# A convolution stem's forward and backward on one core: the planned order of all engines made anew, with leads by chunk

## The chip, the cores and the metric

The kernel runs on one core of a Trainium2 chip. Its time is the device time of one execution in microseconds; of several runs the median counts.

## What is computed

The reference is a strided convolution, a group norm per channel over time, a gelu, and the gradients of all four inputs:

```python
B, T, D, K = 2, 16000, 256, 31;  s = 2;  L = (T - K) // s + 1        # L = 7985
h = sum(jnp.einsum('blc,cd->bld', x[:, i:i + s * L:s, :], w[i]) for i in range(K))
mu = h.sum(1) / L;  var = ((h - mu) ** 2).sum(1) / L
out = gelu((h - mu) / sqrt(var + 1e-5) * gn_gamma + gn_beta)          # tanh form
# returned: out, and the gradients of x, w, gn_gamma, gn_beta for a given grad_out
```

x, w and all results are bfloat16; sums are kept in fp32 in PSUM.

## The kernel before

**The arithmetic.** The sums of products over 31 taps aren't done tap by tap. Taps and positions are split in halves, two and in places three times, and of each split three products are made instead of four or more: of sums or differences of the inputs ("branches" A, B_ and C_, then "leaves" A, B_ and C_). So VectorE forms sums of x, of the gradient and differences of weights, TensorE multiplies, and the shared B_ results are spread to the others in PSUM by VectorE and ScalarE.

**The stages.** F0 and F1: the forward convolution of batch 0 and 1, in four chunks of time c = 0 to 3. Per chunk there are three units (branches). A unit uses two of four PSUM tiles of two banks (`ring`), so its results must be evacuated before the unit after the next begins. `f_three_b` (L616) multiplies, ScalarE copies the product to the other halves of the tile, `f_three_ac` (L634) accumulates on it. `f_seed` (L728) is the VectorE (and for B_ ScalarE) step that adds the B_ results before the last leaves (`f_leaf`, L600) accumulate; `f_evac` (L695) is ScalarE's evacuation with sums for the norm (L711). `f_sums` (L557) holds VectorE's input sums (`tt`, L561), `w_sub` (L549) the weight differences (L551). In F1 the gelu of batch 0 runs beside (`gelu_unit`, L947 on; L956 to L980). G0 and G1: the input gradient of batch 0 and 1, again four chunks, each in two halves of three units, with `g_three_b`, `g_leaf`, `g_three_ac` (all issue from L1162), sums in `g_sums` (L1121), seeds in `g_seed` (L1211; `ve` is L676), and ScalarE's `g_evac` (through `keep`, L691). Beside it run the gelu of batch 1 (in G0), the elementwise gradient (`e_comp`, L1052 on) and differences of the gradient for the weight gradient (`d2_piece`, `sub` L1357), which go to device memory and come back. W: the weight gradient in nine combinations n = 0 to 8 (COMBOS). For each, x tiles of 1 MB are loaded (`x_raw`; two of them added to one, `x_tile`, for some n), gradient tiles come from `d2d` (`d_tile`), and VectorE sums two tiles of x (`w_add`, L1413, also used by `x_tile`), sums pairs of positions (`pair_x`, L1508), forms differences (`pair_d` L1516, `leaf_d` L1587) and spreads products (`w_both`, L1540); TensorE runs `w_pairs`, `w_single` and `w_leaf`, all through L1447. For n = 3 ScalarE's kept products are also stored to `pcd`. For n = 4 the x tiles are made by adding those of n = 2 and n = 3; for n = 5 by adding as well; for n = 6 each of four tiles is two loads and one addition.

**What sets the order.** Nothing is issued while the kernel is being described. Each call of `add` puts an operation in a list: its engine, an assumed duration, what it reads and writes, and its kind (stage, helper and caller, such as "W w_add x_tile"). `Plan.order` (L181) then gives each operation a due time: going backwards, the earliest due time of its users, or its own place on TensorE's axis, less its duration and less a lead that a table holds for its kind. A positive lead makes an operation due earlier. `Plan.listing` (L199) walks through time with a model of the engines and DMA queues and, whenever an engine is free, takes the ready operation that is due first. TensorE may look 13 operations ahead. The result is one fixed order for each engine: TensorE, VectorE (DVE), ScalarE (ACT), GpSimd (POOL) and SyncE (SP), whose order is that of almost all DMA transfers. `emit` (L323) issues all operations in that order and pins them. On the chip each engine takes its instructions in this order and waits for what each one needs.

## Time and profile before

| | |
|---|---|
| median of 3 runs | 1185.56 us (1185.14 to 1185.71) |
| profiled execution, first to last instruction | 1187.8 us |
| TensorE matmul busy | 1149.0 us |
| VectorE busy | 1047.6 us |
| ScalarE busy | 570.0 us |
| mean granted TensorE clock | 0.996 |
| moved by DMA | 255.17 MB, mean 215 GB/s |

The profile is of one execution; for it there is only the span from the first to the last instruction, which is 2.2 us longer than the median time of the unprofiled runs. PE is TensorE's matmul, PEld its weight loads (which overlap), DVE VectorE, ACT ScalarE, POOL GpSimd, SP SyncE. A row of the list of waits tells who waited, for whom, how long in total, how often, and the longest. A row of the timeline has the start, the busy time, engine, line and operation, output and input, how many, and in brackets the idle time ahead of it with what ended it. A row of a stretch has its bounds and length, the busy time and count for PE, PEld, DVE, ACT and POOL, then the granted TensorE clock, the DMA engines' mean busy share and GB/s.

### The profile page before, as it was taken

The numbers are of one execution on the slowest core, as the hardware profiler recorded it, in microseconds if no ns is written. First come the engines' busy times: TensorE is split into PE (matmuls) and PEld (weight loads), VectorE is DVE, ScalarE is ACT, GpSimd is POOL, SyncE is SP. The second block draws the span as 40 slices with busy tenths as digits, with TensorE's granted clock in tenths as the row PEclk, the third lists the DMA queues.
The fourth block names the chain that finished last, engine by engine and source line by source line (L and its number), as shares of the span: only waits on it lengthen the run. The fifth ranks groups of instructions, "written<-read, shape, count | busy, mean of one in ns | idle before, by whom it ended". The sixth has DMA issues, their size and how long they took to land.

```text
span 1187.8 us, 19338 instructions
## 1 busy us (share of the span) xinstructions
PE 1149.0 (97%) x7739; PEld 763.5 (64%) x7796; DVE 1047.6 (88%) x1358; ACT 570.0 (48%) x873; POOL 18.9 (2%) x67
## 2 busy tenths in 40 slices
PE   5999999999999999999999999999999999989998
PEld 3888889777777964444444444444488656656685
DVE  7997898799999989999879997788889898777995
ACT  1254454788885578978884476433322212111200
POOL 0000000000000000000000000000000000000000
PEclk9999999999999999999999999999999999999999
DMA  9446949968986799567639998697998824986774
GB/s 212 73 115 122 200 121 182 205 146 204 204 209 124 270 353 252 167 225 186 221 115 292 270 329 265 161 318 266 317 235 266 271 90 151 359 300 198 239 219 140
DMA packets 334100, 255.17 MB, mean 215 GB/s; under 512 B 187500, under 2 KB 312682, under 8 KB 325738
## 3 DMA queue, kind: packets, MB, share of 16 engines
q1 hardware_dynamic: 333818, 253.93, 76.6%
q8 instruction: 61, 1.00, 0.3%
q14 instruction: 29, 0.24, 0.1%
q0 software_dynamic: 192, 0.00, 0.0%
HBM read 118.95 MB, written 89.62 MB: 176 GB/s over the span
## 4 chain that ended last, share of the span: by engine, by line
PE 46%; DVE 14%; DMA 6%; issue 4%; ACT 1%; SPq 0%; DVEq 0%; ACTq 0%
PE ps L1162 27%; PE ps L1447 15%; PE ps L596 4%; DVE arena L1413 3%; DMA arena<-in_x_dram 2%; DMA arena<-dnd 2%; DVE arena L1357 2%; DVE arena L1587 2%; DVE ps L676 1%; DVE arena L676 1%; DVE arena L1516 1%; DVE arena L1508 1%; DMA dnd<-arena 1%; DVE arena L1121 1%; DVE ps L1540 1%
## 5 line engine op out<-in xcount | busy, mean ns | idle before, releaser
L1162 PE MATMUL ps<-arena 128*128 128x512 bf16 x1974 | 429.7, 376 | 6.6 <-DVE ps L676 3.6
L596 PE MATMUL ps<-arena 128*128 128x256 bf16 (+4 forms) x3460 | 408.2, 281 | 17.8 <-DVE arena L551 7.1
L596 PEld LDWEIGHTS <-arena 128*128 128x128 bf16 x3460 | 338.1, 99 | 87.7 <-DVE arena L551 7.5
L1162 PEld LDWEIGHTS <-arena 128*128 128x128 bf16 x2016 | 197.3, 98 | 237.7 <-issue 6.8
L1447 PE MATMUL ps<-arena 128*128 128x256 bf16 (+1 forms) x2305 | 312.1, 298 | 10.5 <-DVE arena L1508 7.3
L1447 PEld LDWEIGHTS <-arena 128*128 128x128 bf16 x2320 | 228.1, 98 | 94.6 <-DVE arena L1508 8.7
L691 ACT ACTIVATE arena<-ps 128x1024 f32<-128x1024 f32 (+1 forms) x143 | 145.7, 1020 | 285.3 <-PE ps L1447 98.1
L561 DVE TENSOR_TENSOR arena<-arena 128x1087 bf16<-128x1087 bf16 (+3 forms) x211 | 175.5, 866 | 13.7 <-PE ps L596 12.4
L968 DVE TENSOR_TENSOR arena<-arena 128x1024 bf16<-128x1024 bf16 x160 | 107.0, 683 | 8.5 <-ACT arena L962 3.9
L1413 DVE TENSOR_TENSOR arena<-arena 128x4096 bf16<-128x4096 bf16 x38 | 86.3, 2284 | 20.8 <-DMA arena<-in_x_dram 19.5
L1121 DVE TENSOR_TENSOR arena<-arena 128x516 bf16<-128x516 bf16 (+3 forms) x176 | 83.6, 506 | 8.6 <-PE ps L1162 8.0
L676 DVE TENSOR_TENSOR ps<-ps,arena 128x1024 f32<-128x1024 f32 x60 | 73.1, 1224 | 7.9 <-PE ps L1447 4.5
L1357 DVE TENSOR_TENSOR arena<-arena 128x768 bf16<-128x768 bf16 (+3 forms) x112 | 65.4, 636 | 9.9 <-DMA arena<-dnd 4.7
L711 ACT ACTIVATE arena<-ps 128x512 bf16<-128x512 f32 (+1 forms) x64 | 36.9, 578 | 70.4 <-PE ps L596 67.9
L676 DVE TENSOR_TENSOR ps<-arena,ps 128x1024 f32<-128x1024 f32 x44 | 53.8, 1223 | 9.3 <-PE ps L1162 5.5
L1532 ACT COPY ps<-ps 128x256 f32<-128x256 f32 x54 | 19.3, 357 | 78.7 <-PE ps L1447 77.6
L1587 DVE TENSOR_TENSOR arena<-arena 128x2304 bf16<-128x2304 bf16 x36 | 47.4, 1348 | 4.8 <-PE ps L1447 4.8
L1516 DVE TENSOR_TENSOR arena<-arena 128x1024 bf16<-128x1024 bf16 x76 | 48.7, 682 | 1.6 <-DMA arena<-d2d 1.6
L551 DVE TENSOR_TENSOR arena<-arena 128x2048 bf16<-128x2048 bf16 (+1 forms) x52 | 49.8, 989 | 0.0
L958 DVE SCALAR_TENSOR_TENSOR arena<-arena 128x1024 bf16<-128x1024 bf16 x32 | 39.0, 1219 | 11.3 <-ACT arena L956 11.1
L1189 ACT ACTIVATE ps<-ps 128x512 f32<-128x512 f32 x48 | 27.9, 582 | 41.1 <-PE ps L1162 38.0
L1508 DVE TENSOR_TENSOR arena<-arena 128x2048 bf16<-128x2048 bf16 x38 | 45.3, 1216 | 1.2 <-PE ps L1162 1.2
(79 smaller groups left out, 632.8 us busy)
## 6 DMA issues: line engine op xcount, KB each, us to landing
arena<-in_x_dram SPq DMA_DIRECT2D x40, 1024.0 KB, 9.8
arena<-d2d SPq DMA_DIRECT2D x16, 1216.0 KB, 11.5
out_dram<-arena SPq DMA_DIRECT2D x14, 1024.0 KB, 4.4
d2d<-arena SPq DMA_DIRECT2D x30, 384.0 KB, 7.1
arena<-dnd SPq DMA_DIRECT2D x10, 960.0 KB, 5.8
vl<-arena SPq DMA_DIRECT2D x36, 256.0 KB, 3.3
arena<-vl SPq DMA_DIRECT2D x9, 1024.0 KB, 6.8
hd<-arena SPq DMA_DIRECT2D x8, 1024.0 KB, 5.0
```

The source lines that it names most:

```text
L561: lambda: nc.vector.tensor_tensor(out=o, in0=a, in1=b, op=ALU.add))
L596: yield nc.tensor.matmul(ps[:, dh, cs], lhsT=wt, rhs=mv, start=s0, stop=False, skip_group_check=True)
L676: add("DVE", dve(1024, 1), [out], [a, b], lambda: nc.vector.tensor_tensor(out=out, in0=a, in1=b, op=op))
L691: lambda: nc.scalar.activation(out=out, in_=ps, func=ACT.Copy, scale=scale))
L968: add("DVE", dve(1024), [o], [a, b_], lambda: V.tensor_tensor(out=o, in0=a, in1=b_, op=op))
L1121: lambda: nc.vector.tensor_tensor(out=o, in0=a, in1=b, op=ALU.add))
L1162: yield nc.tensor.matmul(ps[:, e, 0:wide], lhsT=lt, rhs=mv, start=s0, stop=False, skip_group_check=True)
L1357: lambda: nc.vector.tensor_tensor(out=out, in0=a, in1=b_, op=ALU.subtract))
L1413: add("DVE", dve(4096), [o], [a, b], lambda: nc.vector.tensor_tensor(out=o, in0=a, in1=b, op=ALU.add))
L1447: yield nc.tensor.matmul(ps[:, s, c0:c1], lhsT=lt, rhs=mv, start=s0, stop=False, skip_group_check=True)
L1516: add("DVE", dve(1024), [d4[:, j]], [d], lambda j=j, o=o, st_=st_: nc.vector.tensor_tensor(out=d4[:, j], in0=d[:, o:o + 3 * st_ + 1:st_, : ...
L1587: add("DVE", dve(2304), [DL[i3, b]], [D2[b]], lambda b=b, i3=i3, o_=o_: nc.vector.tensor_tensor(out=DL[i3, b], in0=D2[b][:, o_:o_ + 17:2, ...
```

## The change

The table of leads is replaced, and a second one, `fine`, is added: for a kind of work it holds further leads by part. The part is the chunk c in the forward pass and the input gradient and the combination n in the weight gradient; it is set in the three loops and noted with every operation. The due time is lessened by both leads. The operations, their durations in the planner, their data and their engines are as before; only the order that `listing` makes of the due times is another.

```diff
         self.lead = {
-            "F0 f_mm f_three_ac": -2.5,
-            "F0 f_mm f_three_b": -4.0,
...
+            "F0 w_sub f_first": -3.5,
+            "F0 w_sub w2_part": -16.5,
...
+            "G1 ve g_seed": 7.0,
...
-            "W w_add x_tile": 3.0,
-            "W w_both weight_grad": 9.0,
...
+            "W load d_tile": -11.0,
...
+            "W w_add x_tile": 4.0,
+            "W w_both weight_grad": 8.0,
...
         }
         self.room, self.mixed = 2048.0, 2.2
         self.overlap = {"DVE": 0.084, "ACT": 0.1}
+        self.fine = {
+            "F0 f_evac last": {0: 8.5, 2: 6.5},
...
+            "F1 ve f_seed": {0: 7.5, 3: -28.5},
...
+            "G1 ve g_seed": {0: -24.5, 1: -27.0, 2: -28.0, 3: -6.5},
...
+            "W leaf_d weight_grad": {0: -10.5, 6: 15.5, 7: -25.5, 8: -41.5},
+            "W load d_tile": {5: -27.5, 6: -39.5, 7: 1.0},
...
+            "W load x_raw": {0: 11.0, 4: 3.0, 5: -4.0, 6: 14.5, 7: 19.5},
...
+            "W w_add x_tile": {3: 8.5, 5: -4.5},
...
+        }
         self.npe = 0
-        self.stage = "F0"
+        self.stage, self.part = "F0", 0
...
-            due[i] = end - full - self.lead.get(o["kind"], 0.0)
+            due[i] = end - full - self.lead.get(o["kind"], 0.0) - self.fine.get(o["kind"], {}).get(o["part"], 0.0)
...
             for c in range(NCK):
+                plan.part = c
...
         for n in range(9):
+            plan.part = n
```

Operations of the weight gradient that make the next combination's x tiles carry the part of the combination in whose loop they are listed: the additions for n = 4 are of part 3.

## The prediction

> **What bounds the kernel now.** I read the page's head first, then TensorE's list of waits, then busy time by stretches, then the timeline where the waits lie. The page's head:

> ```profile
> span 1187.8 us, 19338 instructions
> ...
> PE 1149.0 (97%) x7739; PEld 763.5 (64%) x7796; DVE 1047.6 (88%) x1358; ACT 570.0 (48%) x873; POOL 18.9 (2%) x67
> ```

> TensorE is busy for 1149.0 of 1187.8 us, and its work doesn't change. Only the other 38.8 us can be won by an order. The span is 2.2 us over the median of the three runs (1185.56); I work out differences on the profiled execution and take them off the median. TensorE's waits, longest first (us in total, times, longest):

> ```profile
> PE ps L1447 <- DVE arena L1508: 7.3, 5, 4.2
> PE ps L596 <- DVE arena L551: 7.1, 2, 4.0
> PE ps L596 <- DMA arena<-in_x_dram: 5.8, 2, 4.7
> PE ps L1162 <- DVE ps L676: 3.6, 5, 1.3
> PE ps L596 <- ACT arena L711: 2.3, 4, 0.8
> PE ps L1447 <- DVE ps L1540: 2.0, 3, 1.7
> ```

> The second and third row, 12.9 us, are the start: the first data and the first weight differences. What is left for an order is some 15 us: waits of the weight gradient (L1447) for VectorE's pair sums (L1508) and spread (L1540), of the input gradient (L1162) for seeds (L676), of the forward pass for ScalarE's evacuation (L711). Four stretches show who is loaded (PE, PEld, DVE, ACT, POOL busy, clock, DMA share, GB/s):

> ```profile
> 300.00:350.00 50.00, 50.00 (x379) 36.83 (x378) 50.00 (x73) 44.61 (x69) 1.56 (x4) 1.00 0.89 209
> 470.00:650.00 180.00, 179.10 (x831) 82.81 (x847) 164.57 (x257) 139.21 (x165) 4.99 (x20) 1.00 0.67 201
> 960.00:1010.00 50.00, 47.65 (x339) 33.78 (x339) 45.69 (x41) 10.43 (x18) 0.00 (x0) 0.97 0.47 142
> 1010.00:1060.00 50.00, 44.01 (x305) 30.55 (x306) 35.75 (x24) 8.29 (x12) 0.00 (x0) 0.97 1.05 361
> ```

> From 300 to 650 us TensorE hardly waits (0.0 of 50, 0.9 of 180). From 960 to 1060 it loses 8.3 us, first with VectorE full, then with the DMA engines full (share 1.05, 361 GB/s). The granted clock is down there too; the windows around it (same columns):

> ```profile
> 976.00:979.40 3.40, 3.40 (x19) 2.34 (x17) 3.40 (x4) 0.66 (x1) 0.00 (x0) 0.50 0.75 228
> 1016.70:1021.00 4.30, 2.64 (x25) 2.21 (x23) 2.98 (x3) 0.00 (x0) 0.00 (x0) 1.00 1.08 397
> 1044.30:1047.70 3.40, 3.40 (x17) 2.35 (x16) 2.33 (x2) 0.71 (x2) 0.00 (x0) 0.50 1.09 359
> ```

> Two waits are followed by 3.4 us at half clock, which costs 1.7 us of work each; the third is not.

> **The change part by part.** No instruction is added or removed. In the built program 547 of TensorE's 858 planned groups, 1117 of VectorE's 1326, 501 of ScalarE's 736, 358 of SP's 513 transfers and 10 of GpSimd's 63 stand at another place. A move costs nothing itself; it costs what then waits behind it. I priced the places where TensorE waits now, and those where the new order puts most in front of something that TensorE needs soon.

> *The start: +1.2 us.* TensorE's longer wait for L551, and VectorE's weight differences before it:

> ```profile
> 22.69 1.61 PE L596 MATMUL ps<-arena 128*128 128x256 bf16 x11 [4.05 <-DVE arena L551]
> ```
> ```profile
> 16.88 3.48 DVE L551 TENSOR_TENSOR arena<-arena 128x2048 bf16<-128x2048 bf16 x3
> ```

> The new order puts one more w_sub (3.48/3 = 1.2 us) in front of the one that ends this wait. No later wait of the start could take it back.

> *Evacuations and seeds that get cover: -1.7 and -0.7 us.* Of the four waits for L711, three have more TensorE groups between the evacuated product and the group that reuses the bank: three quarters of 2.3 us. Of the five for seeds, the one at the end of the input gradient has its seed 2.3 us sooner in VectorE's queue: a fifth of 3.6 us.

> *Combination n = 3 of the weight gradient: +2.6 us.* VectorE after 948 us, then at the wait, then TensorE:

> ```profile
> 948.84 2.29 DVE L1413 TENSOR_TENSOR arena<-arena 128x4096 bf16<-128x4096 bf16 x1 [5.05 <-DMA arena<-in_x_dram]
> 951.05 2.35 DVE L676 TENSOR_TENSOR arena<-ps,arena 128x1024 f32<-128x1024 f32 x2
> 953.32 2.28 DVE L1413 TENSOR_TENSOR arena<-arena 128x4096 bf16<-128x4096 bf16 x1
> 955.52 0.68 DVE L1516 TENSOR_TENSOR arena<-arena 128x1024 bf16<-128x1024 bf16 x1
> 956.12 1.22 DVE L1508 TENSOR_TENSOR arena<-arena 128x2048 bf16<-128x2048 bf16 x1
> ```
> ```profile
> 971.86 1.34 DVE L1587 TENSOR_TENSOR arena<-arena 128x2304 bf16<-128x2304 bf16 x1
> 973.13 2.35 DVE L1508 TENSOR_TENSOR arena<-arena 128x2048 bf16<-128x2048 bf16 x2
> ```
> ```profile
> 974.40 0.61 PE L1447 MATMUL ps<-arena 128*128 128x256 bf16 x4 [1.72 <-DVE arena L1508]
> ```

> The product that waits reads both pair_x sums and both leaf_d differences. In the new order three x_tile additions of combination 4 (L1413) move ahead of them, and the leaf_d go behind the pair_x. From 951.1 us there then stand five w_add (2.2 us from start to start), eight ve (1.17), three pair_x (1.17), four pair_d (0.60) and the two leaf_d (1.27): 11.0 + 9.4 + 3.5 + 2.4 + 2.5 = 28.8, so the last leaf_d ends at 979.9 us, where the last pair_x now ends at 975.5: 4.4 us later. One w_single group of 16 matmuls moves ahead of the waiting product as cover; at 0.113 us each (half of 2.04/9, the half-clock row below) that is 1.8 us. Bounds: 0, if VectorE's 5.05 us wait for the x load shrinks, and +4.4 without cover. I take 2.6, since that load still waits for the same addition to free its buffer.

> *Combinations n = 5 and 6: -6.4 us.* VectorE waits for x (DMA), then ends the pair sum late; TensorE waits twice; the two kinds of load (KB each, median us to landing):

> ```profile
> 1015.12 2.29 DVE L1413 TENSOR_TENSOR arena<-arena 128x4096 bf16<-128x4096 bf16 x1 [9.38 <-DMA arena<-in_x_dram]
> ```
> ```profile
> 1042.90 1.22 DVE L1508 TENSOR_TENSOR arena<-arena 128x2048 bf16<-128x2048 bf16 x1
> ```
> ```profile
> 1018.61 0.60 PE L1447 MATMUL ps<-arena 128*128 128x256 bf16 x4 [1.66 <-DVE ps L1540]
> ```
> ```profile
> 1044.18 2.04 PE L1447 MATMUL ps<-arena 128*128 128x256 bf16 x9 [4.17 <-DVE arena L1508]
> ```
> ```profile
> arena<-in_x_dram SPq DMA_DIRECT2D x40, 1024.0 KB, 9.8
> arena<-d2d SPq DMA_DIRECT2D x16, 1216.0 KB, 11.5
> ```

> For the first wait the new order puts a whole w_leaf (16 matmuls of 512 columns, over 3 us) in front of the group that waits: -1.66. For the second, the pair_d and two of the three leaf_d that now run between 1027.6 and 1043 us move behind the last pair_x, and both d2d loads move on SP behind the last x load. From that load's issue at some 1025.5 us, x lands at 1035.3; then two w_add, one leaf_d and the pair_x (2.2 + 2.2 + 1.3 + 1.2) end at 1042.2. The d2d loads, issued just after, land at 1037.5. TensorE arrives at 1040.0 + 2.6 - 1.66 = 1040.9 and waits some 1.2 us, not 4.17, and a wait so short needn't cost clock (1016.7 row): -3.0 - 1.7. Bounds: -7.5 (both waits and the half clock gone) and +1.8 (rival A).

> [...]

> *Seeds elsewhere: +0.7 us.* From 250 to 700 us the new order puts 4 to 17 us of other vector work (gelu, sums, differences) ahead of seeds. In the first batch's input gradient VectorE is idle for 180 - 164.57 = 15.4 us (470:650 row), which hides it if that time comes early enough. The late forward pass has no idle time at all (50.00 of 50). Bounds 0 and +11.9 (rival B); I take one more wait of the mean length, 3.6/5.

> The sum: 1.2 - 1.7 - 0.7 + 2.6 - 6.4 + 0.7 = -4.3; 1185.56 - 4.3 = **1181.3 us**.

> **The rivals.**

> *A, the late wait stays.* DMA is full there (1.05), and what it starts later it lands later. If the chain shifts with combination 3, the last x load leaves 2.6 us later and the d2d loads land at 1040.1, the second 3.4 us on (1216 KB at 361 GB/s); leaf_d and pair_x follow, and TensorE goes on at 1046.0 instead of 1044.2: +1.8 in place of +2.6 - 6.4. Sum 1.2 - 1.7 - 0.7 + 1.8 + 0.7 = +1.3: 1186.9, no difference.

> *B, slower: seeds and sums stand behind vector work pulled ahead that no idle time has absorbed.* It bites where VectorE is full: at the last chunks of the forward pass and at the start of the second batch's input gradient.

> ```profile
> 327.05 2.63 DVE L561 TENSOR_TENSOR arena<-arena 128x1088 bf16<-128x1088 bf16 x4
> ```
> ```profile
> 331.04 2.12 PE L596 MATMUL ps<-arena 128*128 128x256 bf16 x14
> ```
> ```profile
> 650.22 1.23 DVE L676 TENSOR_TENSOR ps<-arena,ps 128x1024 f32<-128x1024 f32 x1 [0.67 <-PE ps L1162]
> 651.35 0.75 DVE L1062 TENSOR_SCALAR arena<-arena,stats 128x2048 bf16<-128x2048 bf16 x1
> ```
> ```profile
> 653.83 1.46 PE L1162 MATMUL ps<-arena 128*128 128x512 bf16 x6
> ```
> ```profile
> L1121 DVE TENSOR_TENSOR arena<-arena 128x516 bf16<-128x516 bf16 (+3 forms) x176 | 83.6, 506 | 8.6 <-PE ps L1162 8.0
> L676 DVE TENSOR_TENSOR ps<-ps,arena 128x1024 f32<-128x1024 f32 x60 | 73.1, 1224 | 7.9 <-PE ps L1447 4.5
> L1357 DVE TENSOR_TENSOR arena<-arena 128x768 bf16<-128x768 bf16 (+3 forms) x112 | 65.4, 636 | 9.9 <-DMA arena<-dnd 4.7
> ```

> At 329.7 us the sums end that the leaf at 331.0 reads. The new order puts 12 vector instructions ahead of the last of them, 7.9 us at 0.66 each. Off that go the margin of 1.3 and 2.6 us of TensorE groups that also move ahead (24 matmuls at 0.113): 4.0 late, with half clock 5.7. At 650.2 the seed gets 16 instructions in front: two scalings (L1062), nine sums (L1121), five differences (L1357): 1.5 + 4.6 + 3.2, less 0.1 overlap each, 7.7 us. Off go the 0.67 us in which VectorE waited and 2.4 us until TensorE's group at 653.8: 4.6 late, with half clock 6.3. Both in full, in place of my 0.7: 1192.6. With the first in full, since VectorE is full there, and half of the second: 1181.3 - 0.7 + 5.7 + 3.1 = 1189.4. It decides from some 5 us not absorbed; below that the kernel isn't slower.

> *C, most waits go.* All of L1508, L676, L711 and L1540 (15.2 us) and both half clocks (3.4) against the start's 1.2: -17.4, 1168.2. For it speaks that the new order treats just these kinds chunk by chunk; against it, the DMA share of 1.05 and the 28.8 us of vector work at combination 3.

> That the order doesn't change is excluded by the counts above.

> **How the numbers follow.** My forecast 0.50 (1181.3), A 0.14 (1186.9), B 0.24 (1189.4), C 0.12 (1168.2). About 0.2%, 2.4 us, is what a measurement of this kernel can tell from no change. Faster by more (under 1183.2) are the forecast and C, 0.62; within it A and the weak end of B, 0.16; slower B, 0.22. The range reaches half way to C and past the middle of B, short of its full price: 1172 to 1191.

> **What would show it.** Right: the start's wait for L551 grows from 7.1 by about 1 us; the wait for L1508 near 974 us is longer than 1.7 and followed by half clock; the one near 1044 shrinks under 2 us and keeps full clock; L1540's nearly goes. Wrong: L1162 or L596 waiting for VectorE by several microseconds between 250 and 700 us (B); the wait near 1044 as long as now (A). The forecast fails if VectorE comes to 250 or 650 us later than I assume, or if SP's new order starts the x loads of combination 6 later.

## The result and the profile after

The changed kernel is slower: median 1190.47 us of 19 runs (1186.98 to 1195.98) against 1185.98 us for the kernel before on the same chip (19 runs, 1184.31 to 1189.12). The ratio is 1.0039, 95% interval 1.0027 to 1.0051, so some 4.6 us. A second set gave 1.0022 (1.0010 to 1.0033). The forecast was 1181.3 us; its range held the median just below its upper end, and its sign was wrong.

The profile doesn't show that loss at first. The head of the page of after, then TensorE's waits (us in total, times, longest):

```profile
span 1185.8 us, 19322 instructions
...
PE 1148.1 (97%) x7740; PEld 762.2 (64%) x7796; DVE 1048.1 (88%) x1358; ACT 569.3 (48%) x873; POOL 21.9 (2%) x67
```
```profile
PE ps L727 <- DVE arena L682: 5.9, 1, 5.9
PE ps L727 <- DMA arena<-in_x_dram: 5.8, 2, 4.7
PE ps L1580 <- DMA arena<-d2d: 4.7, 2, 3.0
PE ps L727 <- ACT ps L763: 4.2, 6, 1.3
PE ps L1580 <- DVE arena L1721: 2.6, 3, 1.5
PE ps L727 <- DVE arena L692: 2.6, 2, 1.9
PE ps L727 <- ACT arena L842: 2.3, 4, 0.8
PE ps L1294 <- DVE ps L807: 1.3, 2, 1.0
```

Line numbers have moved with the longer tables: L727 is the old L596 (the forward pass's products), L1294 the old L1162 (the input gradient's), L682 is the old L551 (weight differences), L692 the old L561 (sums), L763 the old L632 (ScalarE's copies of a B_ product), L807 the old L676 (seeds), L842 the old L711 (evacuation), L1580 the old L1447, L1721 the old L1587 (`leaf_d`). Pair sums (old L1508) and the spread (old L1540), 9.3 us of waits before, are gone from the list (in a second profile of after, below, the pair sums are back with 1.4 us). In their place stand the gradient loads `d2d` (none before) and the `leaf_d`; the copies have gone from 1.2 to 4.2 us, and from 2 waits to 6. The row of before for the copies:

```profile
PE ps L596 <- ACT ps L632: 1.2, 2, 1.0
```

This span is 2.0 us *shorter* than before's 1187.8. Both spans are single executions, and not from the same place among their kernels' runs. A time is the span and some 2 us around it: in the second set the profiled execution of before has the span 1187.8 again and the time 1189.57, against a median of 1186.92; the first profile of after belongs to the 1188.02 run, the second fastest of its 19. By this estimate the forecast's profile, of the same span, was of an execution some 3 us over before's median, too.

To see where the time lies I added up TensorE's axis by stage: from the start of one planned group's weight loads to that of the next, given to the stage of the group (my tabulation, two profiles of each kernel, us):

| | before | before again | after | after again |
|---|---|---|---|---|
| F0 | 215.8 | 215.9 | 217.0 | 215.8 |
| F1 | 209.8 | 209.8 | 213.7 | 214.6 |
| G0 | 170.6 | 171.3 | 171.7 | 171.7 |
| G1 | 264.8 | 264.5 | 261.2 | 262.0 |
| W | 322.8 | 322.3 | 318.2 | 322.7 |

The forward pass of batch 1 (F1) loses 4 to 5 us in both profiles, three of them in chunk 2 (56.7 to 59.8). G1 gains 3. W gains 4.5 in one execution and nothing in the other.

In F1 no single wait is large. TensorE's timeline of after, the rows behind a wait:

```profile
306.58 0.60 PE L727 MATMUL ps<-arena 128*128 128x256 bf16 x4 [0.78 <-ACT arena L842]
...
337.16 0.59 PE L727 MATMUL ps<-arena 128*128 128x512 bf16 x2 [0.73 <-DVE arena L692]
...
354.73 0.49 PE L727 MATMUL ps<-arena 128*128 128x256 bf16 x3 [0.84 <-ACT ps L763]
...
383.18 1.06 PE L727 MATMUL ps<-arena 128*128 128x231 bf16 x9 [1.27 <-ACT ps L763]
...
414.29 0.96 PE L727 MATMUL ps<-arena 128*128 128x231 bf16 x8 [0.80 <-ACT ps L763]
```

And ScalarE at the third of them, in the second profile of after, where it lies 1.2 us earlier:

```profile
350.21 1.06 ACT L1110 ACTIVATE arena<-arena 128x1024 bf16<-128x1024 bf16 x1 [1.63 <-DVE arena L1100]
351.17 0.19 ACT L1110 ACTIVATION_READ_ACCUMULATOR arena<-arena 128x1 f32 x1
351.27 0.36 ACT L763 ACTIVATE ps<-ps 128x256 f32<-128x256 f32 x1
351.57 1.22 ACT L1088 ACTIVATE arena<-arena,stats 128x1024 bf16<-128x1024 bf16 x1
352.70 0.76 ACT L763 ACTIVATE ps<-ps 128x256 f32<-128x256 f32 x2
```

The product that these three copies read was done at 348.9 us. ScalarE first waits 1.63 us for VectorE at an activation of the gelu, runs it, makes one copy, runs another activation (1.22), and makes the other two; TensorE, which has come to the user of the product after 3.5 us of other work, waits for them and goes on at 353.5. In before's order (its second profile) the same product was done at 350.7 us and its user came 7.0 us later. ScalarE's copies stood among activations there too:

```profile
354.48 0.37 ACT L632 ACTIVATE ps<-ps 128x256 f32<-128x256 f32 x1
...
355.82 0.36 ACT L632 ACTIVATE ps<-ps 128x256 f32<-128x256 f32 x1
...
357.25 0.36 ACT L632 ACTIVATE ps<-ps 128x256 f32<-128x256 f32 x1
```

The last of them ended 6.9 us after the product, just in time, so TensorE didn't wait. TensorE's waits for these copies within F1 alone, in before and in the two profiles of after:

```profile
PE ps L596 <- ACT ps L632: 0.2, 1, 0.2
```
```profile
PE ps L727 <- ACT ps L763: 2.9, 3, 1.3
```
```profile
PE ps L727 <- ACT ps L763: 4.0, 4, 1.7
```

That is 2.7 and 3.8 us of the 3.9 and 4.8 that F1 takes longer.

The weight gradient in after: the waits near 864 and 1040 us, and the one at 977 us.

```profile
866.22 2.02 PE L1580 MATMUL ps<-arena 128*128 128x256 bf16 x17 [1.77 <-DMA arena<-d2d]
...
978.87 0.60 PE L1580 MATMUL ps<-arena 128*128 128x256 bf16 x4 [1.46 <-DVE arena L1721]
...
1042.52 5.70 PE L1580 MATMUL ps<-arena 128*128 128x256 bf16 x34 [2.95 <-DMA arena<-d2d]
```

### The profile page after: what moved, and what is told of

It reads as the page before. It is cut to its first block, busy times and chain, and to the rows that moved or that the text cites. A ratio compares the mean times of both kernels' runs of the same rounds, so it can differ in the third digit from the quotient of the medians.

```text
span 1185.8 us, 19322 instructions
## 1 busy us (share of the span) xinstructions
PE 1148.1 (97%) x7740; PEld 762.2 (64%) x7796; DVE 1048.1 (88%) x1358; ACT 569.3 (48%) x873; POOL 21.9 (2%) x67
## 4 chain that ended last, share of the span: by engine, by line
PE 50%; DVE 10%; DMA 5%; ACT 2%; issue 2%; SPq 0%; DVEq 0%; POOL 0%; ACTq 0%
PE ps L1294 31%; PE ps L1580 16%; PE ps L727 4%; DVE arena L1546 3%; DMA arena<-in_x_dram 2%; DMA d2d<-arena 1%; DVE arena L1649 1%; DMA arena<-d2d 1%; DVE arena L1721 1%; DVE arena L1641 1%; DVE ps L1673 1%; DVE arena L807 1%; DMA arena<-dyd 1%; DVE arena L1490 1%; ACT arena L1213 0%
## 5 line engine op out<-in xcount | busy, mean ns | idle before, releaser
L1294 PE MATMUL ps<-arena 128*128 128x512 bf16 (+1 forms) x1974 | 429.4, 377 | 4.4 <-DVE ps L807 1.3
L727 PE MATMUL ps<-arena 128*128 128x256 bf16 (+4 forms) x3460 | 409.9, 281 | 21.2 <-DVE arena L682 5.9
L727 PEld LDWEIGHTS <-arena 128*128 128x128 bf16 x3460 | 338.1, 98 | 92.8 <-issue 13.8
L1294 PEld LDWEIGHTS <-arena 128*128 128x128 bf16 x2016 | 197.3, 98 | 235.3 <-issue 4.1
L1580 PE MATMUL ps<-arena 128*128 128x256 bf16 (+1 forms) x2306 | 309.8, 297 | 8.2 <-DMA arena<-d2d 4.7
L1580 PEld LDWEIGHTS <-arena 128*128 128x128 bf16 x2320 | 226.8, 98 | 91.3 <-issue 4.4
L692 DVE TENSOR_TENSOR arena<-arena 128x1087 bf16<-128x1087 bf16 (+3 forms) x211 | 175.4, 868 | 17.1 <-PE ps L727 16.0
L1100 DVE TENSOR_TENSOR arena<-arena 128x1024 bf16<-128x1024 bf16 x160 | 107.0, 686 | 11.9 <-ACT arena L1092 5.4
L1253 DVE TENSOR_TENSOR arena<-arena 128x514 bf16<-128x514 bf16 (+3 forms) x176 | 83.1, 510 | 14.7 <-PE ps L1294 12.2
L807 DVE TENSOR_TENSOR ps<-ps,arena 128x1024 f32<-128x1024 f32 x60 | 73.3, 1226 | 4.8 <-PE ps L1580 2.5
L842 ACT ACTIVATE arena<-ps 128x512 bf16<-128x512 f32 (+1 forms) x64 | 37.0, 580 | 68.8 <-PE ps L727 65.9
L807 DVE TENSOR_TENSOR ps<-arena,ps 128x1024 f32<-128x1024 f32 x44 | 53.9, 1225 | 10.3 <-ACT arena L1352 4.8
L797 ACT ACTIVATE arena<-ps 128x512 f32<-128x512 f32 x56 | 30.3, 598 | 44.5 <-PE ps L727 28.7
L682 DVE TENSOR_TENSOR arena<-arena 128x2048 bf16<-128x2048 bf16 (+1 forms) x52 | 50.5, 991 | 0.0
L1721 DVE TENSOR_TENSOR arena<-arena 128x2304 bf16<-128x2304 bf16 x36 | 47.8, 1353 | 0.3 <-PE ps L1580 0.2
## 6 DMA issues: line engine op xcount, KB each, us to landing
arena<-in_x_dram SPq DMA_DIRECT2D x40, 1024.0 KB, 8.7
arena<-d2d SPq DMA_DIRECT2D x16, 1216.0 KB, 10.6
out_dram<-arena SPq DMA_DIRECT2D x14, 1024.0 KB, 4.4
arena<-vl SPq DMA_DIRECT2D x9, 1024.0 KB, 7.5
hd<-arena SPq DMA_DIRECT2D x8, 1024.0 KB, 6.1
```

Source lines behind the costliest of these rows:

```text
L692: lambda: nc.vector.tensor_tensor(out=o, in0=a, in1=b, op=ALU.add))
L727: yield nc.tensor.matmul(ps[:, dh, cs], lhsT=wt, rhs=mv, start=s0, stop=False, skip_group_check=True)
L807: add("DVE", dve(1024, 1), [out], [a, b], lambda: nc.vector.tensor_tensor(out=out, in0=a, in1=b, op=op))
L1100: add("DVE", dve(1024), [o], [a, b_], lambda: V.tensor_tensor(out=o, in0=a, in1=b_, op=op))
L1253: lambda: nc.vector.tensor_tensor(out=o, in0=a, in1=b, op=ALU.add))
L1294: yield nc.tensor.matmul(ps[:, e, 0:wide], lhsT=lt, rhs=mv, start=s0, stop=False, skip_group_check=True)
```

## The experiments

The kernel before ran along with each set (medians 1185.7 to 1187.1 us); a ratio is against these runs. Each kernel has its own line numbers, so the text names the operation. Theory 1 at the start was what the table says: the earlier stages lose, the weight gradient gains. Its rival: the weight gradient loses, in most executions, because it hangs on loads.

**Both kernels again**, unchanged.

> The kernel before once more, for a second profile and for the clock and span of each run. Theory 1 (the profiled execution of before was a slow one of its kind): span of about 1183.8 us, that is a time of 1186, with one of the two half-clock stretches of the weight gradient gone or a shorter wait near 1040 us. Theory 2 (the two profiles are typical of their kernels and the profile is not the time that is measured): span of 1187 to 1188.5 again, with both half-clock stretches.

> The changed kernel once more, for a second profile. Its runs so far lie from 1187 to 1196 us, those of before from 1184 to 1189. Theory 1 (the new order has thinner margins, and in some executions a wait of the weight gradient comes back with half clock): the second profile is 1 to 6 us longer than 1185.8, clock 0.994 or less, and the additional time lies in waits for DMA in the weight gradient and half-clock stretches. Theory 2 (the loss is the same in each execution): same waits in the same places, span within 1 us of 1185.8.

Measured: before 1186.92 us (12 runs, 1183.72 to 1190.26), profile with span 1187.8, both half-clock stretches and a wait of 4.6 us near 1040: the waits are in the same places each time, as theory 2 said, though this execution, too, lies above the median. After 1190.9 us (1188.04 to 1193.19), ratio 1.0022, span 1190.8. This profile has 5.0 us more than the first of after, 4.5 of them in W, as the first theory for this run said; F1's share is the same to 0.9 us. So F1's loss is in both profiled executions of after, and W's gain in only one.

**Mixtures of the lead tables.** For a stage the old entries are put back and its `fine` entries dropped, as in

```diff
-            "F1 f_mm f_three_b": -7.5,
-            "F1 f_three_b forward": 5.0,
+            "F1 f_mm f_three_b": -9.5,
+            "F1 f_three_b forward": 4.5,
...
-            "F1 f_mm f_three_b": {0: 3.5, 1: 5.5, 3: -12.0},
```

> New leads, coarse and fine, for the weight gradient alone; the other stages have the old ones. Theory 1 (what the profiles show by stage: TensorE's idle time falls in the weight gradient by 2.3 us and one half clock of 1.7 us goes, and the loss comes from the earlier stages): 2 to 4 us faster than before, 1182 to 1184. Theory 2 (the weight gradient's new order is what loses, because it is at the mercy of the loads): 3 to 5 us slower than before, 1189 to 1191, with a wide spread between runs.

> New leads, coarse and fine, for the forward pass and the input gradient; the weight gradient has the old ones. Theory 1 (the earlier stages lose): 5 to 8 us slower than before, 1191 to 1194. Theory 2 (the weight gradient loses): within 1.5 us of before, 1185 to 1187.5, with before's narrow spread.

> The new leads everywhere, except that all kinds of the forward pass of batch 1 have their old ones. Theory 1 (this stage loses 4 to 5 us and the others together nothing): its share of TensorE's time falls from 214 to about 210 us, and the time to 1186 to 1187.5, level with before. Rival (the loss moves on, since the gelu that this stage no longer pulls ahead is due in the input gradient): the share falls, the next stage's rises from 171.7 by 2 us or more, and the time stays over 1189.

> The new leads, coarse and fine, for the input gradient of batch 1 and the weight gradient; the forward pass and the input gradient of batch 0 have the old ones. Theory 1 (these two stages gain 3 us and 0 to 4 us, and the border between them is covered only when both are new): 3 to 5 us faster than before's 1187, at 1182 to 1184. Rival (the border's wait of 5.4 us with half clock, which the weight gradient's new leads alone brought, stays; the gain belongs to the stage's new order only with the earlier stages' new order): 1186.5 to 1189.

| | median us | ratio, 95% interval |
|---|---|---|
| e_w_only (W new) | 1188.08 | 1.0006 (0.9993 to 1.0019) |
| e_w_old (W old) | 1194.64 | 1.0069 (1.0046 to 1.0092) |
| e_f1_old (F1 old) | 1193.91 | 1.0072 (1.0055 to 1.0089) |
| e_g1w (G1 and W new) | 1209.41 | 1.0198 (1.0181 to 1.0214) |

Theory 1 and the rival of the start both failed on e_w_only, which lies between them. e_w_old lost the 5 to 8 us over before that theory 1 gave it (7.5), but its profile, of an execution 7 us over its median, has near half of its loss in the weight gradient with the old leads (328.5 us against before's 322.8). For e_f1_old the rival was right: the loss moved on, and G0 took 180.4 us in its profile instead of 171.7. For e_g1w neither held. Three of the four are slower than both kernels, and long waits stand in them that neither kernel has. TensorE's timeline in e_w_only at the start of W (for the pair sums), and from the lists of waits of e_f1_old (for a copy in G0) and e_g1w (for seeds in G1):

```profile
864.24 4.02 PE L1474 MATMUL ps<-arena 128*128 128x256 bf16 x18 [5.43 <-DVE arena L1535]
```
```profile
PE ps L1261 <- ACT ps L1288: 5.1, 2, 4.7
```
```profile
PE ps L1214 <- DVE ps L727: 10.8, 4, 7.9
```

A lead moves operations into the neighbouring stage too: what one stage doesn't do is late in the next. So these mixtures don't measure a stage; they make a third order.

**Finished lists spliced.** Both tables are run, each gives its list, and the lists are cut behind the last TensorE product of a stage; the remainder is what isn't issued yet, in the other list's order. At the end of F1 the lists differ by 2.4 us of vector work, at the end of G1 by one `pair_d` and one load.

```diff
-        for i in self.order():
+        lists = {"new": self.order()}
+        self.lead, self.fine = olds, {}
+        lists["old"] = self.order()
+        for which, upto in (("new", ("F0", "F1")), ("old", ("F0", "F1", "G0", "G1", "W"))):   # s_f
+            src = lists[which]
+            cut = 1 + max(k for k, i in enumerate(src) if engine(i) == "PE" and stage(i) in upto)
+            order += [i for i in src[:cut] if i not in done]
...
+        for i in order:
```

> The finished lists are spliced, not the leads: the changed kernel's order up to the last product of the forward pass, from there the order of before (what is not yet issued, in that order). At this cut the two lists differ by a few operations only (2.4 us of vector work). Theory 1 (the loss is the forward pass: 430.5 us of TensorE's axis against 425.7, because VectorE stands idle 40.7 us against 37.0 until its end, with equal work): 3.5 to 5.5 us slower than before's 1187, 1190.5 to 1192.5. Rival (the loss lies in the many waits with half clock of the later stages): within 1.5 us of before.

> Spliced lists: before's order through the forward pass, the changed order through both input gradients, before's order for the weight gradient. Theory 1 (the input gradients gain: 433.5 against 435.6 us, since 5 us more of the second gelu is done while VectorE is idle in the first of them): 1.5 to 3 us faster than before, 1184 to 1185.5. Rival (the stages can't be taken singly, as the mixtures of leads showed, and a misfit at a seam costs 4 us or more): 1190 or more.

> Spliced lists: before's order up to the last product of the input gradient, the changed order for the weight gradient. Theory 1 (the weight gradient's new order gains what the profiles show by combination: 4.5 us in n = 5 less 2 to 3 in n = 4 and 2 in n = 0, and half clock now and then): 1 to 3 us faster than before, 1184 to 1186. Rival (its order wins only in some executions, and n = 0 waits as after the leads of the weight gradient alone, 5.4 us): 1187 to 1190.

> Spliced lists: before's order through the forward pass, the changed order for everything after it. Theory 1 (loss in the forward pass, gains behind it): the two gains together, 3 to 5 us faster than before, 1182 to 1184, and so 7 to 8 us faster than the changed kernel. Rival (gains and losses aren't additive): 1186 or more.

> Spliced lists: the changed order up to the last product of the forward pass of batch 0, from there before's. Theory 1 (the forward pass loses in batch 1, not in batch 0): within 2 us of before's 1187, and TensorE's share of batch 1 within 0.5 us of 209.8. Rival (batch 0's new order leaves VectorE an order of work that starves it at the start of batch 1, and the loss is there whichever order follows): 1190.5 or more, batch 1's share 212 or more.

| changed order in | median us | ratio, 95% interval | F0 | F1 | G0 | G1 | W |
|---|---|---|---|---|---|---|---|
| s_f: F0, F1 | 1192.78 | 1.0056 (1.0038 to 1.0075) | 216.1 | 214.2 | 170.8 | 264.1 | 324.0 |
| s_f0: F0 | 1188.38 | 1.0023 (1.0010 to 1.0036) | 215.8 | 211.0 | 170.6 | 264.1 | 321.1 |
| s_g: G0, G1 | 1190.37 | 1.0038 (1.0022 to 1.0053) | 215.7 | 209.8 | 173.8 | 262.2 | 322.0 |
| s_w: W | 1182.49 | 0.9973 (0.9961 to 0.9985) | 216.8 | 209.8 | 170.6 | 262.9 | 317.4 |
| s_gw: G0, G1, W | 1187.99 | 1.0013 (1.0001 to 1.0025) | 215.6 | 209.8 | 174.2 | 262.7 | 321.4 |

The forward pass loses 6.0 us by the medians. 2.7 of them come with batch 0's order, which makes batch 1 start worse (TensorE waits 1.1 us at 218 us for ScalarE's part of a seed); F1's share shows 1.2 us of that, and the rest isn't seen in the profile of s_f0. The weight gradient gains 4.3 us, though one of the two profiles of after showed no gain in it. So far theory 1 holds. On the input gradients it was wrong: they lose 3.6 us. G1 does gain 2.3, but the first chunk of G0 waits 3 us for a copy and the first combination of W takes 2.4 us more (33.9 against 31.5), as it does in after. **s_w is the best version: 0.9973, faster than both kernels.** s_f came out where theory 1 had it (0.3 us above its range), s_w gained more than either theory gave, s_g and s_gw came out as their rivals said, and s_f0 lies between its two theories. The pieces are good to some 2 us: s_g and s_w add up to -0.7 us by medians and to +1.3 by ratios, and s_gw, which has both, measured +1.2 and +1.5.

**The two places of the input gradients.** ScalarE in s_gw ahead of the late copy, and TensorE:

```profile
439.43 1.00 ACT L905 ACTIVATE arena<-ps 128x1024 f32<-128x1024 f32 x1
440.44 1.28 ACT L1175 ACT_TABLE_LOAD   x1
442.92 1.06 ACT L1175 ACTIVATE arena<-arena 128x1024 bf16<-128x1024 bf16 x1 [1.19 <-DVE arena L1173]
```
```profile
444.51 1.67 PE L1377 MATMUL ps<-arena 128*128 128x512 bf16 x7 [3.11 <-ACT ps L1404]
```

Again the copy stands behind an activation that itself waits for VectorE, and that here has a table load (ACT_TABLE_LOAD, 1.28 us) ahead of it. s_gwfix moves it, and two loads:

```diff
+        for i, after in ((1763, 1762), (2912, 2743)):   # copy behind its product; d_tile behind its store
+            order.remove(i)
+            order.insert(1 + max(order.index(p) for p in {after} | set(self.ops[i]["preds"])), i)
+        order.remove(2913)                              # second d_tile load
+        order.insert(order.index(2973), 2913)           # ahead of an x load
```

> As s_gw (1188.0 us: before's order through the forward pass, then the changed one), with two places put back: in the first chunk of the input gradient ScalarE's copy that TensorE waited 3.1 us for goes directly behind its product (past three activations of the gelu and one evacuation), and SyncE issues the two gradient loads of n = 0 ahead of the x loads that the changed order puts in front of them, as before did. Theory 1 (these two places, 3.1 and 2.4 us with half clock, are what the input gradients' new order loses): 3.5 to 6 us faster than s_gw, 1182 to 1184.5, level with s_w. Rival (the copy moved ahead makes the gelu late, as in e_copies, and the loads wait for the same store anyway): 1187 or more.

Measured 1185.89 us, ratio 0.9992 (0.9976 to 1.0008); s_gw had 1.0013. That is 2.5 us gained, by ratios whose intervals overlap, against the 3.5 to 6 expected. W's first combination went from 35.8 to 32.8 us, most of the way to before's 31.5, and the wait of 2.39 us for the gradient loads is gone, so these loads were the cause there (1.7 us of the 35.8 were half clock behind that wait). Of the copy's wait half came back as a wait for a seed:

```profile
445.80 1.46 PE L1384 MATMUL ps<-arena 128*128 128x512 bf16 x6 [1.55 <-DVE ps L897]
```

**What loses in F1.** Theory 1: VectorE binds the stage. Its idle time in F1 rose with the loss; busy time in F1 before and in the second profile of after (bounds, length, PE, PEld, DVE, ACT, POOL, clock, DMA share, GB/s):

```profile
216.00:429.00 213.00, 211.50 (x1668) 162.68 (x1669) 204.52 (x303) 158.85 (x267) 3.80 (x11) 1.00 0.84 205
```
```profile
218.00:433.00 215.00, 209.43 (x1648) 160.51 (x1646) 200.78 (x295) 157.16 (x260) 3.75 (x11) 1.00 0.86 203
```

8.5 us idle before, 14.2 after. Rival: ScalarE's copies stand at the wrong place. e_copies moves only the copies, in ScalarE's list; the thin kernels leave out most of one addition of the gelu, and so take work from VectorE; m_pe gives TensorE alone its old order in F1; m_f1 gives all engines theirs.

```diff
+        for i in [i for i in order if ops[i]["eng"] == "ACT" and ops[i]["kind"] in copies]:   # e_copies
...
+            order.insert(at, order.pop(k))   # ahead of the gelu and spread rows right in front of it
```
```diff
-            add("DVE", dve(1024), [o], [a, b_], lambda: V.tensor_tensor(out=o, in0=a, in1=b_, op=op))
+            add("DVE", dve(1024), [o], [a, b_], lambda: V.tensor_tensor(
+                out=o[:, 0:1, 0:32], in0=a[:, 0:1, 0:32], in1=b_[:, 0:1, 0:32], op=op)
+                if b == 0 and op == ALU.add else V.tensor_tensor(out=o, in0=a, in1=b_, op=op))
```

> The changed kernel, but ScalarE's copies of the B_ products (forward pass of batch 1, input gradient of batch 0) are moved in ScalarE's order past the activations of the gelu and the spreads of the elementwise gradient that stand right in front of them; 32 copies move, nothing else. Theory 1 (the loss in the forward pass of batch 1 is TensorE waiting for these copies, which stand behind 1.1 us activations): the waits for them fall from 4.2 and 5.4 us in the two profiles to under 2.5 (the one at 381 us stays, its product is issued too late), and the time falls from 1190.7 by 2 to 3.5 us, to 1187 to 1189. Rival (the wait only changes its name: VectorE is as late, so TensorE then waits for sums and seeds): the waits for the copies fall, the time stays within 1 us of 1190.7.

> The changed kernel, leaving out 31/32 of one addition of batch 0's gelu (16 of 80 products and sums of this form; VectorE's 0.69 us each becomes some 0.1), so that VectorE has about 9 us less to do within the forward pass of batch 1. Theory 1 (this stage is bound by VectorE, whose new idle time comes out as TensorE's waits): batch 1's share of TensorE's axis falls from 214.2 to 210.5 or less and the time by 3 us or more. Rival (it is the place of ScalarE's copies in ScalarE's order, whatever VectorE does): the share stays over 213, the time over 1189.

> The kernel before with the same additions left out. Both theories: TensorE waits only 1.4 us in this stage, so its share stays at 209 to 209.8 us and the time falls by 1 us at most.

> The changed kernel; only TensorE's order within the forward pass of batch 1 is that of before (98 places), all other engines' lists are the changed ones. Theory 1 (TensorE's own order is the cause: it puts the user of a B_ product 1.6 to 3.5 us behind the product where before left 6 to 7, and ScalarE's three copies need 3 to 5): the waits for the copies fall from 4.2 to 5.4 us to 2 or less, this batch's share of TensorE's axis from 214.2 to 211.5 or less, the time from 1190.7 by 2 to 4 us. Rival (the lists of VectorE and ScalarE belong to the changed order of TensorE, so TensorE waits for other things instead): the share stays at 213 or more.

> Spliced lists: the changed order through the forward pass of batch 0, before's for batch 1, the changed one behind it. Theory 1 (batch 1's order loses some 3 us, with batch 0's apart): batch 1's share falls from 214.2 to about 211, as with before's lists behind the changed batch 0, and the time by 2 to 4 us to 1187 to 1188.7. Rival (the loss appears later instead, since the lists behind were made for the changed batch 1): 1190 or more.

| | median us | ratio, 95% interval | F1 |
|---|---|---|---|
| e_copies | 1196.62 | 1.0092 (1.0076 to 1.0109) | 219.7 |
| thin_after | 1190.02 | 1.0034 (1.0020 to 1.0049) | 213.1 |
| thin_before | 1186.51 | 1.0005 (0.9990 to 1.0021) | 209.3 |
| m_pe | 1241.02 | 1.0461 (1.0440 to 1.0482) | 264.5 |
| m_f1 | 1189.74 | 1.0030 (1.0016 to 1.0044) | 211.0 |

thin_after fells theory 1: with some 7 us less for VectorE to do in this stage (busy 193.31 in 213 us) TensorE's axis fell by 1.1 us and the copies are as late as ever.

```profile
218.00:431.00 213.00, 208.71 (x1643) 160.06 (x1642) 193.31 (x293) 156.03 (x260) 3.74 (x11) 1.00 0.86 203
```
```profile
PE ps L727 <- ACT ps L763: 4.9, 8, 1.3
```

But what the rival asks for makes it worse. In e_copies the waits for copies fell only from 4.2 and 5.4 us to 3.5; instead TensorE waits longer for sums (2.6 before the move), evacuations (2.3) and a seed. That the gelu, now later, delays these is argued, not shown:

```profile
PE ps L739 <- DVE arena L704: 4.1, 2, 2.2
PE ps L739 <- ACT arena L854: 4.0, 6, 1.6
PE ps L739 <- ACT ps L775: 3.5, 6, 1.3
...
PE ps L739 <- DVE ps L819: 1.4, 1, 1.4
```

And TensorE's old order among the new lists of the others (m_pe) waits for all of them:

```profile
PE ps L828 <- DVE ps L908: 17.8, 5, 6.1
PE ps L828 <- ACT arena L943: 14.4, 7, 5.5
PE ps L828 <- DVE arena L793: 10.9, 3, 7.0
```

Of what was tried, only all engines' lists together take F1 back to 211.0 (m_f1), and that is where batch 0's new order leaves it (s_f0). Even so the kernel's median is just 0.7 to 1.2 us under after's, and its ratio between after's two, because the new lists behind it meet another start: TensorE waits 3.00 us at 446 us for the copy that s_gw waited for, where after waits 0.94, and the first chunk of G0 takes 53.7 us instead of 50.0. So the loss in F1 is shown, and so is that F1's new lists, taken together, make it; the waits for copies are its largest part in the traces. Which single move makes it stays open.

**Combination 5**, the forecast's largest term.

```diff
+        for i in (3217, 3216):                          # the d_tile loads of n = 5
+            order.remove(i)
+            order.insert(order.index(3211) + 1, i)      # one x load earlier
```

> As s_w (1182.5 us: before's order up to the last product of the input gradient, then the changed one), with SyncE's two gradient loads of combination 5 put back ahead of its last x load, where before had them. Theory 1 (the forecast's step failed because the loads that were moved behind the x load land 4 us or more later than it assumed, so TensorE's wait near 1037 us is now for what they bring): the wait of 2.8 us falls to 1.5 or less, without half clock, and the time by 1.5 to 3 us, to 1179.5 to 1181. Rival (the DMA engines are full, what starts earlier pushes the x load back, and the pair sum is late instead, as before): the wait stays at 2.5 us or more, the time at 1182 to 1184.

Measured 1188.39 us, 1.0018 (1.0005 to 1.0032): 5.9 us slower than s_w by the medians, some 5.3 by the ratios. TensorE in s_w, then in s_w5, and the stretch at half clock in s_w5:

```profile
1037.02 0.60 PE L1663 MATMUL ps<-arena 128*128 128x256 bf16 x4 [2.77 <-DVE arena L1804]
```
```profile
1042.83 5.38 PE L1668 MATMUL ps<-arena 128*128 128x256 bf16 x26 [7.82 <-DVE arena L1729]
```
```profile
1037.50:1047.70 10.20, 4.87 (x23) 3.45 (x24) 10.17 (x11) 1.07 (x3) 0.00 (x0) 0.50 1.02 322
```

Its last pair sums, in s_w and in s_w5:

```profile
1036.80 1.22 DVE L1724 TENSOR_TENSOR arena<-arena 128x2048 bf16<-128x2048 bf16 x1
```
```profile
1041.55 1.22 DVE L1729 TENSOR_TENSOR arena<-arena 128x2048 bf16<-128x2048 bf16 x1
```

With two loads of 1.2 MB ahead of the last x load these sums end 4.8 us later. So their place behind the x load is what the new weight gradient needs; both theories had the size wrong, the rival the direction right. This isn't quite before's order: before issued these two loads ahead of the last two x loads, and combinations 4 and 5 together took 80.6 us there, 78.1 in s_w and 83.3 in s_w5. How much of the gain is the move of the loads alone is therefore not shown.

## Why the prediction was wrong

The weight gradient was forecast at +2.6 - 6.4 = -3.8 us and measured at -4.3 (s_w). That the sum fits is in part luck: n = 3 cost less than forecast and n = 5 and 6 gained less. The forward pass was forecast at +0.2 (start, covered evacuations, seeds elsewhere) and measured at +6.0 (s_f). The input gradients were forecast at -0.7 and measured at +3.6 alone (s_g), less in after, where the copy at 446 us waits 0.94 us instead of 3.05.

**The step that failed is "Seeds elsewhere: +0.7 us"**, the only term for what the forward pass behind the start and the first input gradient lose: it looked for that in VectorE's list only, and took one mean wait. In its place the runs showed +6.0 us for the forward pass, and within F1 waits for ScalarE's copies that grew from 0.2 to 2.9 and 4.0 us. Some 7 us less work for VectorE took back only 1.1 us of F1 (thin_after).

- *The start, +1.2.* The wait for the weight differences grew from 4.05 to 5.95 and 5.24 us, more than forecast, but the wait ahead of it, for differences before and now for sums, shrank from 3.06 to 1.86 and 1.85. The four waits of the start together went from 12.95 to 13.63 and 12.63 us, that is +0.7 and -0.3. "No later wait could take it back" was true; an earlier one did.
- *Evacuations, -1.7.* There are four waits of 2.3 us in all, as before, but none at the products that waited before: the four are at others (one is the 306.58 row). The forecast compared TensorE's order only at the places that waited before. *Seed, -0.7:* the waits fell from 3.6 to 1.3 and 2.3 us, so the direction was right and the gain larger.
- *n = 3, +2.6.* The wait is now for the last `leaf_d`, as worked out (L1721), at 1.46 and 2.15 us, with 1.13 us more close behind it in the first profile and 0.67 in the second. Combinations 3 and 4 together went from 75.7 and 75.6 us to 76.0 and 78.4, so +0.3 to +2.8; in s_w, +0.3. Half clock followed in one profile of two.
- *n = 5 and 6, -6.4.* The first wait went, as forecast. The second shrank from 4.17 to 2.95 and 3.68 us, not to 1.2, and kept its half clock. It waits for the second d2d load (1042.52 row), which landed 17.1 and 17.9 us after the issue of the x load ahead of it, where the forecast took 12: issued at 1029.2 us in the second profile, it landed at 1045.8, 16.6 us later; in the first profile the DMA engines' share from 1025.4 to 1042.5 us was 0.93. The median landing time of 11.5 us wasn't the price there. TensorE also came to this wait 14.3 us after the x load's issue, where the forecast had 15.4, so it waited longer for that reason too. The two combinations gained 4.7 and 3.6 us.
- *What had no term.* ScalarE's copies, whose 1.2 us of waits stood in before's list and were not quoted: in the whole kernel they came to 4.2 and 5.4. The d2d loads of n = 0, each behind one more x load than before: 1.8 and 2.2 us. G1's gain of 3 us.
- *Rival B* named the right stage for a loss, about the right sum (5.7 us, 1.7 of them half clock that F1 didn't have) and, for it, the wrong engine; its second place, the start of G1, lost nothing. So it was luck that its 1189.4 us came nearest to the median.
- *The profile as base.* It was an execution with both half clocks, some 3 us over before's median. Waits that such an execution shows are partly not there to be won in the others.

By the medians the splices add up to 6.0 + 3.6 - 4.3 = +5.3 us, by their ratios to 6.6 + 4.5 - 3.2 = +7.9, against 4.6 and 2.6 measured for the whole. The copy's wait at the start of G0, 2.1 us shorter in after than in s_g, is part of the difference; how the rest divides is open.

## What to carry to other kernels

When an order is redone, walk the path of each product to its user over every engine on it, the lightly loaded ones too: ScalarE was busy for 48% of the span (73% of F1) and still made TensorE wait, since a copy of 0.4 us stood behind an activation that waited for VectorE. Lists of several engines are one object: taken alone, ScalarE's copies cost 6 us and TensorE's list in one stage 50 us over after, and one pair of stages' leads 23 us over before, while cutting finished lists where both have done nearly the same work told roughly which stages lose, and gave a version faster than both (s_w, 0.9973). And take more than one profile of a kernel whose runs spread by 0.4 to 0.8% before you count on a wait.

## What the runs showed of the hardware

```profile
439.86:443.27 3.41, 1.64 (x9) 0.75 (x8) 3.01 (x4) 1.85 (x3) 0.00 (x0) 1.00 1.09 279
443.27:446.68 3.41, 2.13 (x10) 0.97 (x10) 3.41 (x6) 3.41 (x5) 0.00 (x0) 1.00 0.37 149
```
```profile
444.00:447.41 3.41, 1.16 (x6) 0.57 (x6) 3.41 (x5) 2.75 (x4) 0.00 (x0) 1.00 0.64 264
447.41:450.82 3.41, 3.41 (x10) 1.19 (x9) 3.41 (x5) 3.35 (x5) 0.62 (x1) 0.50 0.21 78
```

In s_g 1.77 us of idle time fall into the first and 1.28 into the second, which ran at 1.00; in m_f1 2.25 us fall into one, and the next ran at 0.50. In before the stretch from 972.60 held 2.25 us (the 1.72 at 974.40 and 0.53 behind it), and the next ran at 0.50; the stretch from 1016.97 held 1.64 us, nearly all of the 1.66 at 1018.61, and the next ran at 1.00. The granted clock also goes with the spread: the 14 runs of before with a mean granted clock of 0.997 took 1185.4 us in the mean, the 12 with 0.994 took 1187.8. And it is part of the loss: the mean granted clock of 41 runs of before was 0.9955, of 31 runs of after 0.9943, which on 1190 us is, by estimate, some 1.4 us.
